# Retention, expert routing and two MLPs on one core: conversion steps, gate halves and weight splits in another order

## The chip, the cores and the metric

One core of a Trainium2 chip runs the whole program. The engines are PE (matrix products; PEld is its loading of weights), DVE (vectors, reads matmul results), ACT (scalar functions and copies), POOL (GpSimd; elementwise work and indirect DMAs) and SP (issues the other DMAs). Each engine runs its own instructions in the order in which the program wrote them, and waits for others through semaphores. The metric is the device time of the program in microseconds (us), the median of several runs; lower is better.

## The reference

```
scores = q @ k^T / 8                      # 8 batches, 8 heads, 576 positions, width 64
x = (scores * D) @ v                      # D[i, j] = gamma_h ** (i - j) for i >= j, else 0; no softmax
logits = x @ w_gate                       # x as 4608 tokens x 512; 8 experts
# greedy: pairs (token, expert) by falling logit; a token is taken once, an expert takes 576 tokens
out[mask_e] = relu(x[mask_e] @ w1[e]) @ w2[e]        # each expert, width 1024
h = relu(out @ w_in); result = (h * h) @ w_out       # one MLP for all tokens, width 2048
```

## The kernel before

All of it is float32; a product of high precision is made of three products of split operands (high part, low part).

**Attention** (`attention`) goes over 36 tiles of 128 tokens, `for t in range(NT)`. A tile's work is cut up by hand and written a tile or two ahead of its use: `turn_k(t + 2)` transposes keys on PE into the bank `pr` and ACT copies them out (line 145, `kT`); `scores(t + 1)` makes the scores of the next tile in two banks `sc` (165), which DVE empties as it multiplies by the decay mask (169, `A`; in each ninth tile a memset behind each, 171); `before(t)` and `values(t)` make the tile's result in `px` (197, 205), which ACT copies to `X` (208, written as `big`); `state(t)` updates the running state (179, and on DVE 183 or 185, `S`). POOL scales queries and keys (152, 155).

The **gate** logits of four tiles at a time come from `gate(t0, t1)`, a generator in two halves. The first multiplies by the gate's weights into `pr` (127) and ACT copies the bank to `gs` (130), which has one buffer; the second transposes `gs` on PE into `pr` again (134) and DVE adds the four parts into `L` (135). `pr` is one bank: each user waits until the one before has been copied out.

**Conversion** (`convert`, the generator `filler`): the weights of the last MLP arrive as float64 and are made into float32 in 32 units. One `next(filler)` is a step, and a unit goes through several: the load in step s, three ACT instructions in step s + 2 (561 to 563), three DVE instructions in step s + 3 (567 to 569), the store to DRAM in step s + 5. Each step so works on several units, with one unit's ACT part and another's DVE part in it. The loop takes one step a tile; what is left is done behind attention.

**The router's first part** (`rt.prep(0, 32)`, two halves) is written at tiles 34 and 35; behind the loop stand the gates of tiles 32 to 34 and of tile 35 (the latter in the bank `sp`), and `rt.prep(32, 36)`. `rt.start()` writes ten DVE instructions once, at tile 3 (358 to 361).

**Then** the threshold search for the first expert runs on DVE and PE (398 to 435), while PE turns `X` back and SP stores it to DRAM (`turn_back`, 658 to 662). `pump()` moves the weight stream: it splits one fetched chunk if it may (`raw` into `w1`, `w2`: ACT 628, POOL 629, DVE 630) and issues the fetch of one more; two chunks may be fetched ahead and three split ahead. `pump(True)` only fetches. When the first expert's token list is ready, POOL gathers its rows by index (`gather`, 708, one instruction a block), PE transposes each block (`turn`, 716), and the expert's products start once three of five blocks are turned (`moe`, 802 then 785). Meanwhile PE is given 36 transposes of nothing (896). In `moe(0)` one `pump()` stands behind each of 16 chunks' use.

Of the kernel before, what the change touches and what calls it, by code (L numbers as in the profile page):

```python
# [6 lines left out]
F32 = mybir.dt.float32  # L7
# [8 lines left out]
NT = 36  # L16
# [53 lines left out]
def attention(tc, a, X, idn, rt, filler):  # L70
# [3 lines left out]
    with ExitStack() as c:  # L74
        cn = c.enter_context(tc.tile_pool(name="acn", bufs=1))
        wk = c.enter_context(tc.tile_pool(name="awk", bufs=2))
# [3 lines left out]
        def load(t, w0=0, w1=3):  # L80

            src = a["att"][t].rearrange("p (w g i) -> p w g i", w=3, g=4)
            if w0 == 0:
                T[t] = wk.tile([128, 2, 4, 128], F32, name="qk", bufs=5)
                nc.sync.dma_start(T[t], src[:, :2])
            if w1 == 3:
                V[t] = wk.tile([128, 4, 128], F32, name="v", bufs=4)
                nc.sync.dma_start(V[t], src[:, 2])
# [33 lines left out]
        def gate(t0, t1, bank="pr"):  # L122

            n, o = t1 - t0, 128 * (t0 % 4)
            p = ps.tile([128, 512], F32, name=bank)
            for g in range(4):
                nc.tensor.matmul(p[32 * g:32 * g + 32, :128 * n], wg[:, g, :], X[t0 // 4][:, g, o:o + 128 * n],
                                 start=True, stop=True)
            gs = wk.tile([128, 512], F32, name="gs", bufs=1)
            nc.scalar.activation(gs[:, :128 * n], p[:, :128 * n], AF.Copy)  # L130
            yield
            p = ps.tile([128, 512], F32, name=bank).rearrange("p (t c e) -> p t c e", t=4, c=4)
            for i in range(n):
                nc.tensor.transpose(p[:, i], gs[:, 128 * i:128 * i + 128], idn)
            nc.vector.tensor_reduce(L[:, t0:t1, :], p[:, :n, :, :NE].rearrange("p t c e -> p t e c"),
                                    axis=AX.X, op=OP.add)
            yield

        def turn_k(t):

            p = ps.tile([128, 512], F32, name="pr").rearrange("p (g i) -> p g i", g=4)
            for g in range(4):
                nc.tensor.transpose(p[:, g], T[t][:, 1, g, :], idn)
            K[t] = wk.tile([128, 4, 128], F32, name="kT")
            nc.scalar.activation(K[t], p, AF.Copy)

        def weigh(t):

            ph, d = t % 9, D[t]
            if ph != 0:  # L150
                d["qh"] = wk.tile([128, 4, 128], F32, name="qh")
                nc.gpsimd.tensor_mul(d["qh"], T[t][:, 0], qc[:, ph])
            if ph != 8:
                kh = wk.tile([128, 8, 64], F32, name="kh")
                nc.gpsimd.tensor_mul(kh, T[t][:, 1].rearrange("p g (h d) -> p (g h) d", h=2),
                                     kc[:, ph, :].unsqueeze(2).to_broadcast([128, 8, 64]))
                d["kh"] = kh.rearrange("p (g h) d -> p g (h d)", h=2)
# [42 lines left out]
        def values(t):  # L200
            ph, px = t % 9, P[t]
            for g in range(4):
                for i in range(2):
                    lo, o = 64 * i, 64 * (i ^ g % 2)
                    nc.tensor.matmul(px[o:o + 64, g, :], V[t][:, g, lo:lo + 64], D[t]["A"][i][:, g, :],  # L205
                                     start=(ph == 0), stop=True)
            o = 128 * (t % 4)
            nc.scalar.activation(X[t // 4][:, :, o:o + 128], px, AF.Copy)
# [4 lines left out]
        def logits():  # L213
            for t in range(0, 32, 4):
                yield from gate(t, t + 4)
# [7 lines left out]
        for t in range(NT):  # L223
            if t + 2 < NT:
                turn_k(t + 2)
            if t + 1 < NT:
                weigh(t + 1)
                scores(t + 1)
            if t + 5 < NT:
                load(t + 5, 0, 2)  # L230
            if t + 3 < NT:
                load(t + 3, 2, 3)
            if t + 2 < 9:
                decay(t + 2)
            before(t)
            if t >= 4 and t % 2 == 0:
                next(todo, None)
            values(t)
            if t % 9 != 8:
                state(t)  # L240
            if t == NT - 2:
                ready = rt.prep(0, 32)
            if t >= NT - 2:
                next(ready)
            if t == 3:
                rt.start()
            next(filler, None)
        last = [gate(32, 35), gate(35, 36, "sp")]
        for g in last:
            next(g)  # L250
        for g in last:
            next(g)
        for _ in rt.prep(32, 36):
            pass

# [329 lines left out]
def body(tc, a, out):  # L585
    nc = tc.nc
    with ExitStack() as ctx:
# [10 lines left out]
        with tc.tile_pool(name="cv", bufs=2) as cv:  # L598
            filler = convert(nc, a, cv, wd)
# [4 lines left out]
        wk = ctx.enter_context(tc.tile_pool(name="wk", bufs=2))  # L604
# [6 lines left out]
        ev, near, listed = {}, set(), set()  # L611
# [8 lines left out]
        def pump(fetch_only=False):  # L620

            i = st["split"]
            if i < st["fetched"] and i < st["used"] + 3 and not fetch_only:
                raw = raws.pop(i)
                w1 = wk.tile([128, 2, 512], R, name="w1", bufs=3)
                w2 = wk.tile([128, 2, 512], R, name="w2", bufs=5)
                for w, c in ((w1, raw[:, :512]), (w2, raw[:, 512:])):
                    nc.scalar.activation(w[:, 0], c, AF.Copy)  # L628
                nc.gpsimd.tensor_sub(w1[:, 1], raw[:, :512], w1[:, 0].bitcast(F32))  # L629
                nc.vector.tensor_sub(w2[:, 1], raw[:, 512:], w2[:, 0].bitcast(F32))  # L630
                chunks[i] = (w1, w2)
                st["split"] += 1
            i = st["fetched"]
            if i < len(stream) and i < st["split"] + 2:
                kind, k, f = stream[i]
                if kind == "e" and k not in ev:
                    return
                raw = raws[i] = wk.tile([128, 1024], F32, name="raw", bufs=2)
                nc.sync.dma_start(raw, wd[f] if kind == "m"
                                  else a["we"][bass.ds(ev[k], 1), f].rearrange("o p c -> (o p) c"))  # L640
                st["fetched"] += 1
# [103 lines left out]
        def route():  # L745
            for k in range(NE):
                yield from rt.phase(k)

        router, loader = route(), load_tokens()
# [138 lines left out]
        while 0 not in listed:  # L888
            long = next(router) == "long"
            for _ in range(1 + long):  # L890
                next(turner, None)
            pump(0 not in near)
        assert next(turner, None) is None
        warm = ps.tile([128, 512], F32, name="mm", bufs=3)
        for _ in range(36):
            nc.tensor.transpose(warm[:, :128], idn, idn)
        while state["turned"] < 3:
            next(loader)
        pump()
# [27 lines left out]
```

## Time and profile before

| | us |
|---|---|
| three runs: lowest, median, highest | 1529.21, 1531.27, 1531.87 |
| the profiled execution's own time | 1525.86 |
| its span | 1524.1 |
| PE busy of the span | 1462.2 (96%) |
| DVE, ACT, POOL busy | 963.5, 675.0, 468.5 |
| attention, up to the last copy to `X` | 0 to 169.5 |
| search for the first expert's list, `X` stored | about 172 to 206 |
| first gather issued; first expert product | 208.19; 218.00 |
| first expert (two parts of 8 chunks) | 218 to 280 |

A row of the timeline is one or some equal instructions: start, duration, engine, line, operation, what it writes and reads, and in brackets how long its engine sat idle before it and what ended that. A row of groups gives the count, the summed busy time and the mean in ns of one. A row of windows gives the busy time of each engine in a stretch, the granted share of TensorE's clock (1.00 is 2.4 GHz, 0.50 is 1.2 GHz) and what the DMA engines moved.

### The profile page before, as it was taken

The page shows a single profiled execution, that of the slowest core. Times are in us where ns is not written, and L with a number is a line of the kernel's source. Part 1 is how long each engine was busy: PE and PEld are TensorE (multiplying, and loading weights), DVE is VectorE, ACT ScalarE, POOL GpSimd, SP SyncE. Part 2 cuts the span into 40 slices and gives each one's busy share as a digit, 9 for nine tenths or more (in the row PEclk, how much of TensorE's full clock was granted, in tenths as well). Part 3 has the DMA queues.
Part 4 walks back from the last instruction along what each step waited for, and adds up shares of the span by engine and source line. Part 5 has one row for each costly group of instructions (what it writes and reads, how often), then busy time and mean ns, then how long its engine had stood idle before and what let it go on. Part 6 is the DMA issues. An engine that isn't in the chain of part 4 may idle for free.

```text
span 1524.1 us, 27399 instructions
## 1 busy us (share of the span) xinstructions
PE 1462.2 (96%) x10599; PEld 1324.4 (87%) x10599; DVE 963.5 (63%) x1965; ACT 675.0 (44%) x1349; POOL 468.5 (31%) x410
## 2 busy tenths in 40 slices
PE   7998879999999999999999999999999999999997
PEld 6777768888988898889988899899888999999896
DVE  5999768766765657557765667567646455454341
ACT  6766644444433434334433344344334344444332
POOL 4454134544312224124213143233122431242110
PEclk9999979999999999999999999999999999999999
DMA  9999567224511224225313143234112351252110
GB/s 337 347 365 352 197 203 257 97 70 133 158 56 72 87 93 154 70 97 157 107 56 96 58 148 127 68 123 161 56 61 89 123 174 64 64 180 95 57 49 21
DMA packets 64210, 201.14 MB, mean 132 GB/s; under 512 B 8400, under 2 KB 8656, under 8 KB 64080
## 3 DMA queue, kind: packets, MB, share of 16 engines
q1 hardware_dynamic: 58128, 179.99, 35.2%
q0 software_dynamic: 5952, 19.40, 3.6%
q8 instruction: 83, 1.36, 0.4%
q14 instruction: 47, 0.39, 0.1%
HBM read 172.10 MB, written 27.26 MB: 131 GB/s over the span
## 4 chain that ended last, share of the span: by engine, by line
PE 73%; DVE 11%; DMA 6%; issue 5%; ACT 4%; POOL 0%; SPq 0%; ACTq 0%; DVEq 0%; POOLq 0%
PE mm L865 24%; PE acc L849 23%; PE acc L785 9%; PE mm L802 8%; DMA raw<-we 4%; DVE w L630 3%; PE px L205 2%; ACT w L628 1%; PE sc L165 1%; PE mm L716 1%; PE rps L508 1%; DVE cb L569 1%; DVE G L398 1%; DVE A L169 1%; DMA raw<-wd 1%
## 5 line engine op out<-in xcount | busy, mean ns | idle before, releaser
L629 POOL TENSOR_TENSOR w<-raw,w 128x512 fp32r<-128x512 f32 x212 | 278.0, 1311 | 825.8 <-ACT w L628 729.0
L630 DVE TENSOR_TENSOR w<-raw,w 128x512 fp32r<-128x512 f32 x212 | 265.4, 1252 | 228.7 <-ACT w L628 224.4
L628 ACT ACTIVATE w<-raw 128x512 fp32r<-128x512 f32 x424 | 243.3, 621 | 205.7 <-DMA raw<-we 163.0
L849 PE MATMUL acc<-big,h 128*128 128x512 f32 x972 | 246.0, 397 | 0.0
L785 PE MATMUL acc<-h,w 128*128 128x288 f32 x1536 | 224.4, 296 | 12.0 <-DVE YL L792 9.7
L785 PEld LDWEIGHTS acc<-h,w 128*128 128x128 f32 x1536 | 208.4, 188 | 14.6 <-DVE YL L792 11.6
L849 PEld LDWEIGHTS acc<-big,h 128*128 128x128 f32 x972 | 180.1, 188 | 35.4 <-DVE h L842 0.3
L871 ACT ACTIVATE r<-mm 128x384 f32<-128x384 f32 x192 | 93.9, 489 | 237.7 <-PE mm L865 217.2
L875 ACT ACTIVATE h<-r 128x384 fp32r<-128x384 f32 x192 | 100.9, 525 | 216.8 <-DVE r L873 216.8
L849 PE MATMUL acc<-w,h 128*128 128x512 f32 x756 | 190.9, 396 | 2.9 <-DVE h L842 2.9
L873 DVE TENSOR_TENSOR r<-mm,r 128x384 f32<-128x384 f32 x192 | 105.9, 551 | 125.5 <-ACT r L871 125.3
L865 PE MATMUL mm<-YH,big 128*128 128x384 f32 x864 | 173.4, 342 | 0.0
L849 PEld LDWEIGHTS acc<-w,h 128*128 128x128 f32 x756 | 139.3, 188 | 29.6 <-DVE h L842 3.7
L802 PE MATMUL mm<-XH,w 128*128 128x288 f32 x1024 | 161.0, 300 | 0.8 <-ACT XH L724 0.7
L865 PEld LDWEIGHTS mm<-YH,big 128*128 128x128 f32 x864 | 152.1, 188 | 7.7 <-ACT YH L791 0.9
L842 DVE TENSOR_TENSOR h<-r,h 128x384 fp32r<-128x384 f32 x192 | 110.9, 577 | 65.7 <-ACT h L875 65.7
L802 PEld LDWEIGHTS mm<-XH,w 128*128 128x128 f32 x1024 | 143.8, 190 | 2.0 <-ACT XH L724 1.1
L865 PE MATMUL mm<-YH,w 128*128 128x384 f32 x672 | 133.3, 339 | 0.0
L865 PEld LDWEIGHTS mm<-YH,w 128*128 128x128 f32 x672 | 117.6, 188 | 4.3
L865 PE MATMUL mm<-YL,big 128*128 128x384 f32 x432 | 93.4, 338 | 0.0
L802 PE MATMUL mm<-XL,w 128*128 128x288 f32 x512 | 89.0, 295 | 0.0
L865 PEld LDWEIGHTS mm<-YL,big 128*128 128x128 f32 x432 | 77.3, 188 | 0.3 <-DVE YL L792 0.2
(171 smaller groups left out, 1713.5 us busy)
## 6 DMA issues: line engine op xcount, KB each, us to landing
raw<-we SPq DMA_DIRECT2D x128, 512.0 KB, 3.6
raw<-wd SPq DMA_DIRECT2D x84, 512.0 KB, 3.2
qk<-att SPq DMA_DIRECT2D x36, 512.0 KB, 7.0
craw<-wm SPq DMA_DIRECT2D x32, 512.0 KB, 6.7
v<-att SPq DMA_DIRECT2D x36, 256.0 KB, 5.4
wd<-cb SPq DMA_DIRECT2D x32, 256.0 KB, 5.4
xd<-YH SPq DMA_DIRECT2D x18, 256.0 KB, 3.5
xd<-YL SPq DMA_DIRECT2D x18, 256.0 KB, 3.6
```

Of the source, the lines that this page charges most:

```text
L205: nc.tensor.matmul(px[o:o + 64, g, :], V[t][:, g, lo:lo + 64], D[t]["A"][i][:, g, :], start=(ph == 0), stop=True)
L628: nc.scalar.activation(w[:, 0], c, AF.Copy)
L629: nc.gpsimd.tensor_sub(w1[:, 1], raw[:, :512], w1[:, 0].bitcast(F32))
L630: nc.vector.tensor_sub(w2[:, 1], raw[:, 512:], w2[:, 0].bitcast(F32))
L785: nc.tensor.matmul(acc[part][d][:, :288], w2[:, wi, d * 128:(d + 1) * 128], h[:, xi, :288], start=(f == 0 and i == 0), stop=(f == 7 and i ...
L802: nc.tensor.matmul(p[:, :288], w1[:, wi, g * 128:(g + 1) * 128], X[xi][:, g, 288 * part:288 * part + 288], start=(g == 0 and i == 0), stop ...
L842: nc.vector.tensor_sub(h[:, 1], s, h[:, 0].bitcast(F32))
L849: nc.tensor.matmul(acc[t], h[:, xi, t * 128:(t + 1) * 128], w2[:, wi], start=(f == 0 and i == 0), stop=(f == 15 and i == 2))
L865: nc.tensor.matmul(p[:, :384], w1[:, wi, g * 128:(g + 1) * 128], Y[xi][:, g, o:o + 384], start=(g == 0 and i == 0), stop=(g == 3 and i == 2))
L871: nc.scalar.activation(r, p[:, :384], AF.Relu)
L873: nc.vector.tensor_mul(s, p[:, :384], r)
L875: nc.scalar.activation(h[:, 0], s, AF.Copy)
```

## The change

```diff
-            gs = wk.tile([128, 512], F32, name="gs", bufs=1)
+            gs = wk.tile([128, 512], F32, name="gs", bufs=2)
...
             before(t)
-            if t >= 4 and t % 2 == 0:
+            if t >= 4 and t % 4 < 2:
                 next(todo, None)
+            if t == NT - 1:
+                last = gate(32, 35)
+                next(last)
             values(t)
             if t % 9 != 8:
                 state(t)
-            if t == NT - 2:
+            if t == NT - 3:
                 ready = rt.prep(0, 32)
-            if t >= NT - 2:
+            if NT - 3 <= t < NT - 1:
                 next(ready)
+            if t == NT - 1:
+                next(last)
             if t == 3:
                 rt.start()
-            next(filler, None)
-        last = [gate(32, 35), gate(35, 36, "sp")]
-        for g in last:
-            next(g)
-        for g in last:
-            next(g)
+            for _ in range(1 + (t in (12, 20, 28))):
+                next(filler, None)
+        for _ in gate(35, 36, "sp"):
+            pass
         for _ in rt.prep(32, 36):
             pass
...
             for _ in range(1 + long):
                 next(turner, None)
-            pump(0 not in near)
+            pump(True)
         assert next(turner, None) is None
         warm = ps.tile([128, 512], F32, name="mm", bufs=3)
         for _ in range(36):
             nc.tensor.transpose(warm[:, :128], idn, idn)
+        for _ in range(4):
+            next(loader)
+        pump()
         while state["turned"] < 3:
             next(loader)
         pump()
```

Tiles 12, 20 and 28 take two conversion steps. With the change the last ACT part of the conversion is written at tile 30 (before: 33), the last DVE part at tile 31 (34), the last store at tile 33 (behind the loop). A gate's second half stands one tile behind its first (before: two), so at tiles 5, 9, ... 33 (6, 10, ... 34). The gate of tiles 32 to 34 has its first half ahead of `values(35)` and its second behind it. The first two chunks of weights are no longer split ahead of the gathers: the first split stands behind four gathers, the second behind three turned blocks, and in `moe(0)` each chunk is then split one chunk later than before.

ACT at tiles 20 and 21, before (208 copies tile 20's result, 561 to 563 are a unit's conversion, 145 copies the keys of tile 23, the next 208 is tile 21):

```order
L130 ACTIVATE gs<-pr 128x512
L208 ACTIVATE big<-px 128x4x128
L561 ACTIVATE cb<-craw 128x512
L562 ACTIVATE cn<-craw 128x512
L563 ACTIVATE cn<-cn 128x512
L145 ACTIVATE kT<-pr 128x512
L208 ACTIVATE big<-px 128x4x128
```

The same place with the change, whose conversion lines are numbered three higher:

```order
L130 ACTIVATE gs<-pr 128x512
L208 ACTIVATE big<-px 128x4x128
L564 ACTIVATE cb<-craw 128x512
L565 ACTIVATE cn<-craw 128x512
L566 ACTIVATE cn<-cn 128x512
L564 ACTIVATE cb<-craw 128x512
L565 ACTIVATE cn<-craw 128x512
L566 ACTIVATE cn<-cn 128x512
L145 ACTIVATE kT<-pr 128x512
L208 ACTIVATE big<-px 128x4x128
```

A second unit stands ahead of the keys' copy out of `pr`, which the gate's second half of tile 21 now follows on PE in the same bank.

DVE from the state of tile 20 to that of tile 21, with the change (570 to 572 are 567 to 569 of before, where one conversion stood and no 135):

```order
L185 TENSOR_TENSOR S_129<-sp,S_128 128x256
L570 TENSOR_SCALAR cs<-cb 128x512
L571 SCALAR_TENSOR_TENSOR cs<-cb,cs 128x512
L572 ISA cb<-cs,cn 128x1024
L570 TENSOR_SCALAR cs<-cb 128x512
L571 SCALAR_TENSOR_TENSOR cs<-cb,cs 128x512
L572 ISA cb<-cs,cn 128x1024
L169 TENSOR_TENSOR A_1710<-sc_1700,mask 128x512
L171 MEMSET A_1710 64x4x64
L169 TENSOR_TENSOR A_1711<-sc_1701,mask 128x512
L171 MEMSET A_1711 64x4x64
L135 TENSOR_REDUCE L<-pr 128x32
```

Two conversions now stand ahead of the masks that empty the score banks, and the gate's addition behind them.

POOL from the last query scaling of attention on, as a difference (629, now 632, is a chunk's subtraction into `w1`; 708, now 711, a gather):

```order
 L152 TENSOR_TENSOR qh<-qk,qc 128x512
-L629 TENSOR_TENSOR w_3213<-raw,w_3213 128x512
-L629 TENSOR_TENSOR w_3243<-raw,w_3243 128x512
-L708 DMA xg<-xd,idx 128x512
-L708 DMA xg<-xd,idx 64x512
-L708 DMA xg<-xd,idx 128x512 x3
```

The same place with the change:

```order
L152 TENSOR_TENSOR qh<-qk,qc 128x512
L711 DMA xg<-xd,idx 128x512
L711 DMA xg<-xd,idx 64x512
L711 DMA xg<-xd,idx 128x512 x2
L632 TENSOR_TENSOR w_3280<-raw,w_3280 128x512
L711 DMA xg<-xd,idx 128x512
L632 TENSOR_TENSOR w_3311<-raw,w_3311 128x512
```

The two subtractions that stood ahead of the gathers have moved behind the fourth and the fifth.

## Rows read from the trace of the kernel before

**Rows 1.** Windows by stage: attention, wait for the gathers, first expert

```profile
25.00:150.00 125.00, 115.58 (x1876) 92.14 (x1868) 114.83 (x188) 88.71 (x164) 65.42 (x51) 1.00 0.98 350
...
198.00:218.00 20.00, 11.43 (x91) 9.70 (x89) 11.54 (x38) 5.03 (x10) 7.89 (x7) 0.69 0.62 204
218.00:276.00 58.00, 53.67 (x401) 51.27 (x402) 51.80 (x114) 28.36 (x57) 26.57 (x19) 0.96 0.59 205
```

**Rows 2.** Timeline of PE, keys' transposes in tiles 20 and 21

```profile
103.97 0.66 PE L143 MATMUL pr<-idn,qk 128*128 128x128 f32 x4
...
107.74 0.66 PE L143 MATMUL pr<-idn,qk 128*128 128x128 f32 x4
```

**Rows 3.** Groups by line on DVE, 20 to 172 us

```profile
L169 DVE TENSOR_TENSOR A<-sc,mask 128x512 f32<-128x512 f32 x66 | 42.3, 677 | 2.7 <-PE sc L165 2.7
...
L569 DVE CUSTOM_DVE_ANT_0 cb<-cs,cn 128x1024 uint16<-128x1024 uint16 x32 | 29.9, 936 | 4.4 <-ACT kT L145 0.5
L567 DVE TENSOR_SCALAR cs<-cb 128x512 int32<-128x512 int32 x32 | 26.0, 811 | 0.0
L568 DVE SCALAR_TENSOR_TENSOR cs<-cb,cs 128x512 int32<-128x512 int32 x32 | 22.1, 692 | 1.1
```

**Rows 4.** Timeline of ACT in tile 20, conversion and keys' copy

```profile
104.12 0.67 ACT L561 ACTIVATE cb<-craw 128x512 f32<-128x512 f32 x1
...
105.97 0.58 ACT L145 ACTIVATE kT<-pr 128x512 f32<-128x512 f32 x1
```

**Rows 5.** Timeline of DVE, first and last instruction of `rt.start()`

```profile
27.40 0.27 DVE L358 MEMSET OH<- 128x256 uint32 x1
...
30.21 0.17 DVE L361 CAST OH<-rt 128x32 f16<-128x32 f32 x1
```

**Rows 6.** Timeline of PE, the scores behind that burst

```profile
33.77 1.75 PE L165 MATMUL sc<-qk,kT 64*128 64x128 f32 x16 [1.00 <-DVE A L169]
```

**Rows 7.** Timeline of PE, behind the gate's second half at tile 30

```profile
149.44 0.66 PE L143 MATMUL pr<-idn,qk 128*128 128x128 f32 x4 [1.70 <-DVE L L135]
```

**Rows 8.** Timeline of PE, gate of tiles 32 to 34, first half

```profile
168.73 0.85 PE L127 MATMUL pr<-big,wg 128*32 128x384 f32 x8
```

**Rows 9.** Timeline of ACT, the copy of tile 35's gate

```profile
170.84 0.28 ACT L130 ACTIVATE gs<-sp 128x128 f32<-128x128 f32 x1 [0.70 <-PE pr L134]
```

**Rows 10.** Timeline of POOL, subtractions, first and third gather

```profile
204.92 2.97 POOL L629 TENSOR_TENSOR w<-raw,w 128x512 fp32r<-128x512 f32 x2 [42.38 <-DVE OH L502]
208.19 1.13 POOL L708 DMA_INDIRECT xg<-xd,idx  x1 [0.30 <-DVE U L523]
...
210.86 0.97 POOL L708 DMA_INDIRECT xg<-xd,idx  x1 [0.30 <-issue]
```

**Rows 11.** Timeline of DVE, index copies and a chunk's subtraction

```profile
206.88 1.03 DVE L514 TENSOR_TENSOR idx<-ids 128x4 int32<-128x4 f32 x1
207.83 0.14 DVE L515 TENSOR_TENSOR idx<-ids 64x1 int32<-64x1 f32 x1
...
209.09 0.69 DVE L630 TENSOR_TENSOR w<-raw,w 128x512 fp32r<-128x512 f32 x1
```

**Rows 12.** Timeline of PE from the idle transposes to the first expert

```profile
205.73 5.79 PE L896 MATMUL mm<-idn 128*128 128x128 f32 x36
211.93 0.66 PE L716 MATMUL mm<-idn,xg 128*128 128x128 f32 x4 [0.40 <-DMA xg<-xd,idx]
...
216.22 1.09 PE L716 MATMUL mm<-idn,xg 128*128 128x128 f32 x4 [0.92 <-DMA xg<-xd,idx]
218.00 2.29 PE L802 MATMUL mm<-XH,w 128*128 128x288 f32 x8 [0.69 <-ACT XH L724]
```

**Rows 13.** Windows: the stretch in which the clock was halved

```profile
216.00:222.80 6.80, 5.89 (x24) 5.51 (x25) 4.00 (x8) 2.71 (x6) 1.28 (x1) 0.50 0.20 57
```

**Rows 14.** Timeline of POOL, subtraction of the sixth chunk's `w1`

```profile
231.39 1.30 POOL L629 TENSOR_TENSOR w<-raw,w 128x512 fp32r<-128x512 f32 x1 [3.98 <-ACT w L628]
```

**Rows 15.** Timeline of PE, the sixth chunk's first products

```profile
236.18 1.30 PE L802 MATMUL mm<-XH,w 128*128 128x288 f32 x8
```

## The prediction, written before the changed kernel had run

> **What bounds the kernel now.** I read the windows by stage first, to see which engines are full where the change lies. In the body of attention PE is busy 115.58 of 125 us and DVE 114.83 [rows 1]: both 92%, so neither has time to give away. PE's own timeline then says what a tile costs it: from one transpose of keys to the next in a tile without gate work are 107.74 - 103.97 = 3.77 us, with its five groups of matmuls back to back [rows 2]. DVE needs as much: a conversion is 0.81 + 0.69 + 0.94 = 2.44 us, two masks are 1.35, together 3.79, and the state's update comes on top [rows 3]. So attention is a loop of PE and DVE in which both are the bound, and only tiles with gate work, where PE takes longer, give DVE a pause. Between 198 and 218 us the picture turns: PE is busy 11.43 of 20 us, part of it with transposes of nothing, and waits for the gathers [rows 1, 12]. From 218 to 276 us the first expert uses its 16 chunks, 58 / 16 = 3.6 us each, PE 93% and DVE 89% busy [rows 1]. Behind that PE is 96% busy over the whole span, and I take every microsecond won or lost ahead of it to be kept to the end.
>
> **Double conversion steps (tiles 12, 20, 28): +7.2.** Nothing is added in all; three conversions move from tiles 32 to 34 forward. In each of the three tiles DVE has one conversion more, 2.44 us [rows 3], ahead of the masks that empty the score banks, and PE's next scores wait for these. ACT has one more too, ahead of the copy of the keys out of `pr`: from the conversion's start to the keys' copy are 105.97 - 104.12 = 1.85 us [rows 4], so the gate's second half, now in the very next tile and in the same bank, finds `pr` taken 1.85 us longer. This wait lies beside DVE's and I don't count it again. A bound from below comes from the one burst of extra DVE work that the trace has: `rt.start()` keeps DVE from 27.40 to 30.38, 3.0 us, and PE's scores behind it waited 1.00 us [rows 5, 6]; a tile with a first gate half stood between. The upper bound is the conversion and the keys' transpose, which now has to wait for the gate's addition behind the masks and comes out in series with the scores: 2.44 + 0.66 = 3.1 us [rows 2, 3]. I take 2.4 for each, nearer to the upper end, since ACT and DVE are late in the same tile: 3 x 2.4 = 7.2, bounds 3.0 and 9.3. What hides a part is DVE's pause in a first-half tile, and all three are such tiles.
>
> **The tiles that lose their conversion (32 to 34): 0.** DVE gets lighter there, but a tile costs PE 3.77 us all the same. Bounds: nothing, and one conversion's 2.44 us gained. The loads and stores of the three units move too; the DMA engines were 98% occupied in the body of attention at 350 GB/s [rows 1], but loads are issued several tiles ahead, so I take nothing for this.
>
> **Second gate halves one tile sooner: -1.7 and +0.6.** At tile 30 DVE's addition stood behind two masks and two memsets, and PE's next transpose waited 1.70 us [rows 7]. The second half moves to tile 29, without memsets: -1.7. Against it, tiles with gate work now stand in pairs, and so do those without. Two plain tiles in a row leave DVE behind PE (3.79 and an update against 3.77): between 0 and some 0.3 us for each of four groups of four tiles that have no double step; half of it, +0.6.
>
> **The end of attention: +0.1.** The gate of tiles 32 to 34 now stands on PE ahead of `values(35)`; its 0.85 us [rows 8] used to lie beside ACT's copy of tile 35 and now delays that copy. In exchange tile 35's gate no longer waits 0.70 us for the one buffer [rows 9]. The router's halves on DVE move to tiles 33 and 34, where there is room, and I count nothing for them. Up to here 7.2 - 1.7 + 0.6 + 0.1 = **+6.2 us**.
>
> **Gathers ahead of the splits: -3.3.** POOL's two subtractions last until 204.92 + 2.97 = 207.89, and the first gather follows at 208.19 [rows 10]. The index copies were done at 207.97, but late: one of them took 1.03 us beside these subtractions, the next, alone, 0.14, and a chunk's subtraction on DVE stood ahead of them [rows 11]. The last matmuls of the list end about when the idle transposes start, 205.73 [rows 12]; with four short copies behind them the first gather can go at about 206.7 (an estimate from the 0.14 and the 0.30 that POOL takes from one gather to the next), 1.5 us sooner. What counts is the third gather, since the expert starts with three blocks. It came 2.67 us behind the first, so now at 209.4, and leaves POOL at 210.3. PE turned the first block 2.6 us behind POOL's end (211.93 - 209.32) and the third 4.4 us (216.22 - 211.83) [rows 10, 12]; the fetches of two more chunks, issued as the splits freed their buffers, ran beside it, and these now come later. With 2.6 the third block turns at 212.9, by when the idle transposes (to 211.52) and two turns are over: 3.3 us sooner, and the expert's first product with it, at 214.7 for 218.00. With 4.4 it is 1.5. If the turn also runs as fast as the first one (0.66 for 1.09 us) it is 3.7. I take 3.3.
>
> One rule speaks against this part. The split's subtraction on DVE now runs while POOL issues gathers; in the trace before it did so too, at 209.09 for 0.69 us, and the first gather took 1.13 us where the third took 0.97 [rows 10, 11], so 0.16 is the price seen. The Trainium skill, "SBUF — State Buffer", section "Who interferes with whom", says that an instruction of DVE with two SBUF inputs and one of GpSimd that reads SBUF exclude each other for their whole length; by that the index copy's 1.03 us is explained, and a gather could be held for the whole 0.69 us, the gain would be 2.6 and the sum +3.9.
>
> **Weights one chunk later in the first expert: +0.3.** The sixth chunk's `w1` was ready at 231.39 + 1.30 = 232.69 and used at 236.18, 3.5 us ahead [rows 14, 15]; one chunk takes 3.6. So the weights arrive about when PE wants them. The whole chain of splits starts as much sooner as the expert does. I take 0.3; bounds 0, and 3 if PE waits for weights in most chunks.
>
> **Sum.** +6.2 - 3.3 + 0.3 = **+3.2 us**. The profiled execution took 1525.86, 5.4 below the median of the runs shown; on that median it is 1531.27 + 3.2 = **1534.5 us**.
>
> **Rivals.** *The double steps are absorbed* (the other side). If DVE's pause in the first-half tile takes up most of the second conversion, as the burst suggests, a double step costs 1.0: 3.0 - 1.7 + 0.1 = 1.4, and with -3.3 - 1.6 for the expert's start the result is -3.5, 1527.8. The 1.6 is the clock: it fell to 0.50 from 216 to 222.8 us [rows 13], after PE had mostly waited for gathers, and the turn of the third block took 1.09 for 0.66 us [rows 12]. With less waiting it may not fall; the first expert's products from 218.00 on stood in that stretch, and half of its 6.8 us is 3.4, of which DVE's own work leaves perhaps half. For it: that burst. Against it: the burst cost 1.00 with a pause on both sides, and ACT is late as well. The point that decides is whether a double step costs PE under 1.5 us. The Trainium skill, "TensorE: Matmul & The Clock Gate", section "Why this matters for your kernels", asks for no long idle gaps between matmuls to keep the high clock; the fall at 216 agrees with it, and by it this rival's 1.6 us would come. Chance 0.17.
>
> *The weights are late* in the first expert: the start of the expert moves, its end doesn't, since each chunk now has one use less of lead. Then the 3.3 us are lost and the result is +6.2, 1537.5. For it: 3.5 us of lead against 3.6 for a chunk. Against it: the fetches are issued by the splits and start sooner too. Chance 0.13.
>
> *Nothing changes*: double steps at about 1.5 and a gain of 1.5 to 3.3 at the gathers cancel, 1531 to 1532. Chance 0.12.
>
> **Chances and range.** The forecast, between 0 and +6.5, holds 0.58; its own range is 1531.5 to 1537.5. What a measurement can tell from no change is about 0.2%, 3.1 us, and the forecast lies on that bound: of its 0.58 I give 0.33 to slower and 0.25 to the same. With the late weights slower has 0.46, with the third rival and a little of the first the same has 0.39, faster has 0.15. The range reaches to the first and second rival: 1527.5 to 1539.
>
> **What would show it.** PE idle of some 2 us in tiles 13, 21 and 29, ended by DVE's masks or the gate's addition or ACT's keys; the 1.70 us of tile 30 gone; the last copy to `X` some 6 us later than before; the first gather about 1.5 us closer to the end of the list's matmuls and the expert's product 9 us behind them for 12.3; no wait of PE for `w1`. It would be wrong if DVE's pauses hide the second conversions, or if the weights set the pace of the first expert.

## The result, and the profile after

The changed kernel takes 1537.89 us (median of 9 runs, 1534.44 to 1540.77), the kernel before 1529.54 beside it (9 runs, 1522.35 to 1533.53): ratio 1.0057, 95% interval 1.0038 to 1.0076, so **slower by 8.4 us** (5.8 to 11.6). The forecast was 3.2 us slower, with a range to 1539.0: right in sign and inside the range, short by 5 us.

The profiled execution of the changed kernel took 1540.16 us, with a span of 1538.4. That is 14.3 above the span of before, far more than the medians differ: the first profile of before lies near the low end of its kernel's times. A second profile of the same kernel, taken later (it is the last experiment below), has a span of 1532.6. Both stand in the tables from here on, and what differs between these two is no work of the change.

The windows by stage of the changed kernel answer to [rows 1]. Columns after the stretch: its length, the busy time of PE, PEld, DVE, ACT and POOL, the granted clock, the DMA share, GB/s.

```profile
25.00:150.00 125.00, 111.85 (x1770) 89.19 (x1768) 113.56 (x182) 88.21 (x162) 62.72 (x48) 0.97 0.95 341
208.00:226.00 18.00, 10.83 (x93) 9.60 (x92) 10.38 (x38) 3.94 (x8) 6.32 (x6) 0.81 0.56 184
226.00:286.00 60.00, 54.22 (x401) 51.91 (x402) 52.21 (x113) 27.01 (x57) 25.68 (x19) 0.94 0.63 210
```

In the same 125 us of attention PE's instructions are 1770 for 1876, and the clock is 0.97 for 1.00: attention lost time, and part of that by the clock. The first expert behind it runs at 0.94 for 0.96. What each stage took, in us, from the start of the row that ends it to that of the next (last copy of the normalised tokens to `X`; end of the list's last matmul; first product of the first expert; end of its last L802, L805 after; first product of the second expert, which ends the first shared MLP; end of the span):

| Stage ends with | before | before, second profile | after |
| --- | --- | --- | --- |
| last copy to `X` | 168.9 | 170.4 | 178.6 |
| list's last matmul | 37.0 | 36.9 | 38.4 |
| first product, expert 1 | 12.1 | 11.8 | 8.9 |
| last first-layer product, expert 1 | 57.7 | 62.3 | 59.8 |
| first product, expert 2 | 83.0 | 83.4 | 86.9 |
| end | 1165.4 | 1167.8 | 1165.7 |

Attention is 8.2 to 9.7 longer, the way from the list to the expert 2.9 to 3.2 shorter, the stage that holds the first shared MLP 3.5 to 3.9 longer. The 1.4 us more up to the list's last matmul are not charged to the change: this profile has 0.50 from 182.26 to 189.09 us there, and all other profiles take 36.1 to 37.6. Four groups of rows carry the rest of the text.

**A double step.** ACT and PE behind tile 20, timelines of the changed kernel. ACT copies the second conversion's words, waits for DVE (0.52), and comes to the copy of the keys at 112.77:

```profile
110.36 0.65 ACT L564 ACTIVATE cb<-craw 128x512 f32<-128x512 f32 x1
111.53 0.67 ACT L565 ACTIVATE cn<-craw 128x512 f32<-128x512 uint16 x1 [0.52 <-DVE cb L572]
112.24 0.63 ACT L566 ACTIVATE cn<-cn 128x512 int32<-128x512 f32 x1
112.77 0.58 ACT L145 ACTIVATE kT<-pr 128x512 f32<-128x512 f32 x1
```

```profile
110.08 0.67 PE L197 MATMUL px<-qh,S 64*64 64x128 f32 x16
113.41 0.66 PE L134 MATMUL pr<-idn,gs 128*128 128x128 f32 x4 [2.66 <-ACT kT L145]
113.99 1.98 PE L205 MATMUL px<-A,v 128*64 128x128 f32 x16
115.75 1.07 PE L179 MATMUL sp<-v,kh 128*64 128x64 f32 x16
```

PE, which in [rows 2] goes from one tile to the next without a pause, waits 2.66 us for those keys, since the gate's second half wants their bank. And behind the wait the same 16 matmuls of L205 take 1.98 us, where they take 1.09 elsewhere in attention. Windows of the granted clock behind the three double steps of this kernel (columns as above):

```profile
76.45:79.86 3.41, 3.41 (x38) 2.96 (x34) 2.60 (x6) 1.79 (x4) 0.87 (x1) 0.50 0.78 284
114.00:117.41 3.41, 3.41 (x36) 3.29 (x36) 2.83 (x8) 1.39 (x3) 0.43 (x1) 0.50 0.94 366
151.54:154.96 3.42, 3.42 (x36) 3.00 (x34) 2.12 (x5) 0.70 (x2) 0.00 (x0) 0.50 0.78 308
```

At 0.50 of 2.4 GHz, 3.4 us do the work of 1.7.

**The gathers.** POOL and PE of the changed kernel, timelines, for [rows 10, 12]:

```profile
218.33 1.26 POOL L711 DMA_INDIRECT xg<-xd,idx  x1 [46.71 <-DVE nn L530]
219.89 0.91 POOL L711 DMA_INDIRECT xg<-xd,idx  x1 [0.30 <-issue]
221.10 0.97 POOL L711 DMA_INDIRECT xg<-xd,idx  x1 [0.30 <-issue]
```

```profile
216.85 5.56 PE L899 MATMUL mm<-idn 128*128 128x128 f32 x36
222.25 1.17 PE L719 MATMUL mm<-idn,xg 128*128 128x128 f32 x8
224.60 0.63 PE L719 MATMUL mm<-idn,xg 128*128 128x128 f32 x4 [1.18 <-DMA xg<-xd,idx]
225.91 1.71 PE L805 MATMUL mm<-XH,w 128*128 128x288 f32 x8 [0.69 <-ACT XH L727]
```

From the start of the idle transposes to the third block's turn are 7.75 us for 10.49 (10.58 in the second profile of before). That turn takes 0.63 for 1.09, but 0.63 in the second profile of before too, so this part is no effect of the change. The first gather, with the split's subtraction on DVE beside it (218.60, 0.69 us), takes 1.26 where the next two take 0.91 and 0.97: some 0.3 us, and not the 0.69 that the prediction drew from the Trainium skill, "SBUF — State Buffer", "Who interferes with whom". The same section also says that a `tensor_tensor`, which this subtraction is, was not seen to stall DMAs; the 0.3 us lie between the two.

**The first shared MLP.** DVE and PE of the changed kernel, timelines:

```profile
296.86 1.38 DVE L633 TENSOR_TENSOR w<-raw,w 128x512 fp32r<-128x512 f32 x1 [1.63 <-ACT w L631]
298.16 1.64 DVE L845 TENSOR_TENSOR h<-r,h 128x384 fp32r<-128x384 f32 x1
...
302.68 1.36 DVE L633 TENSOR_TENSOR w<-raw,w 128x512 fp32r<-128x512 f32 x1 [1.64 <-ACT w L631]
303.97 1.62 DVE L845 TENSOR_TENSOR h<-r,h 128x384 fp32r<-128x384 f32 x1
```

```profile
299.86 1.90 PE L852 MATMUL acc<-big,h 128*128 128x512 f32 x7 [0.82 <-DVE h L845]
...
305.64 1.89 PE L852 MATMUL acc<-w,h 128*128 128x512 f32 x7 [1.21 <-DVE h L845]
```

A chunk's subtraction (L633) stands ahead of the low half of the activations (L845), and PE's second layer waits for that, twice. Both are long here: POOL's subtractions of the same split and of a kept chunk of the last MLP's weights lie beside them (296.39 to 299.38), and where POOL subtracts nothing L633 takes 0.69 (218.60) and L845 0.56 (306.65). In the kernel before, PE's timeline shows no wait in the same steps (276 to 300 us). Splits are made while they lead by less than three chunks; the changed kernel enters this stage with a lead of two, so its first step, which takes a chunk that was kept in SBUF and so uses up none of the stream, makes one split more.

### The profile page after: what moved, and what is told of

It is laid out like the page before. It is cut to its first block, busy times and chain, and to the rows that moved or that the text cites. A ratio compares the mean times of both kernels' runs of the same rounds, so it can differ in the third digit from the quotient of the medians.

```text
span 1538.4 us, 27395 instructions
## 1 busy us (share of the span) xinstructions
PE 1468.5 (95%) x10599; PEld 1330.9 (87%) x10599; DVE 966.9 (63%) x1965; ACT 674.6 (44%) x1349; POOL 468.4 (30%) x410
## 4 chain that ended last, share of the span: by engine, by line
PE 69%; DVE 13%; DMA 7%; issue 5%; ACT 4%; POOL 0%; SPq 0%; ACTq 0%; DVEq 0%; POOLq 0%
PE mm L868 24%; PE acc L852 23%; PE acc L788 6%; PE mm L805 6%; DMA raw<-we 6%; DVE w L633 4%; PE px L205 2%; ACT w L631 2%; PE sc L165 1%; DVE G L401 1%; PE rps L511 1%; PE mm L719 1%; DVE cb L572 1%; PE mm L661 1%; PE pr L143 1%
## 5 line engine op out<-in xcount | busy, mean ns | idle before, releaser
L633 DVE TENSOR_TENSOR w<-raw,w 128x512 fp32r<-128x512 f32 x212 | 267.6, 1262 | 232.1 <-ACT w L631 226.8
L788 PE MATMUL acc<-h,w 128*128 128x288 f32 x1536 | 225.0, 297 | 15.8 <-DVE YL L795 12.1
L805 PE MATMUL mm<-XH,w 128*128 128x288 f32 x1024 | 161.3, 300 | 0.9 <-ACT XH L727 0.7
L845 DVE TENSOR_TENSOR h<-r,h 128x384 fp32r<-128x384 f32 x192 | 112.0, 583 | 65.0 <-ACT h L878 65.0
L805 PEld LDWEIGHTS mm<-XH,w 128*128 128x128 f32 x1024 | 144.0, 190 | 1.9 <-ACT XH L727 0.9
L805 PE MATMUL mm<-XL,w 128*128 128x288 f32 x512 | 89.1, 296 | 0.0
```

Source lines behind the costliest of these rows:

```text
L788: nc.tensor.matmul(acc[part][d][:, :288], w2[:, wi, d * 128:(d + 1) * 128], h[:, xi, :288], start=(f == 0 and i == 0), stop=(f == 7 and i ...
L805: nc.tensor.matmul(p[:, :288], w1[:, wi, g * 128:(g + 1) * 128], X[xi][:, g, 288 * part:288 * part + 288], start=(g == 0 and i == 0), stop ...
L845: nc.vector.tensor_sub(h[:, 1], s, h[:, 0].bitcast(F32))
```

## The experiments

Each was timed in five rounds against the kernel before on the same chip; the ratios are to that, and microseconds are the ratio times 1531. L numbers shift with the lines of each kernel.

**Single steps, all else as changed.**

```
-            for _ in range(1 + (t in (12, 20, 28))):
+            for _ in range(1):
```

> The change with one conversion step in every tile, all else as in the change. Theory: the double steps are the whole loss; each costs some 3.7 us, 2.7 of them PE's wait for the keys' copy and the rest the halved clock behind that wait. Without them attention's last copy to X comes at about 169, as before, PE's clock stays at 1.00 in attention, and the kernel is 3 to 4 us faster than before, some 11 us faster than the change. Rival: the doubles cost the 2.4 us each that was forecast and the rest comes from the search and the first expert; then this kernel stays 2 to 3 us slower than before.

Ratio 1.0011 [0.9995, 1.0027]. Against the changed kernel's 1.0057 the double steps are worth 7.0 us, with some 4 us to either side. No stretch at half clock stands in attention before 168 us. Stages: 171.1, 37.6, 8.8, 58.8, 86.5, 1166.3. The expected gain of 3 to 4 us over the kernel before didn't come, though the way from the list to the expert took 8.8 us.

**Gathers ahead of the splits alone** (the second part of the diff on the kernel before).

> The kernel before with the gathers ahead of the weight splits alone. Theory: the first expert's product comes 3 us sooner after the list's last matmuls (9.0 for 12.1 us), and the gain is kept: 3 us faster than before, 1527 for 1530. Rival, late weights: the first expert's end does not move or comes later, since each chunk is split one chunk later; then within 1 us of before, or up to 4 us slower, as the second half of the first expert in the profile after (4 us longer than before) would have it.

Ratio 1.0012 [0.9995, 1.0029]: no gain, so the time is the rival's, but not for its reason, since the first expert is not longer. Stages: 170.5, 36.9, 8.9, 55.6, 86.1, 1167.0. Its first product comes 3.2 us closer to the list, and the first expert keeps that; the clock is 1.00 from the expert's first product on, and the first eight matmuls take 1.32 us for the 2.29 of [rows 12]. But the MLP's stage is 3 us longer, by the same two waits. PE's timeline of this kernel at both places:

```profile
216.35 1.32 PE L802 MATMUL mm<-XH,w 128*128 128x288 f32 x8 [0.69 <-DVE XL L725]
...
285.17 1.90 PE L849 MATMUL acc<-big,h 128*128 128x512 f32 x7 [0.82 <-DVE h L842]
290.96 1.90 PE L849 MATMUL acc<-w,h 128*128 128x512 f32 x7 [1.22 <-DVE h L842]
```

**The attention part alone** (the changed kernel with splits and gathers as before).

> The change with the weight splits ahead of the gathers as before, so the attention part alone. Theory: all of the loss is here, 9 to 11 us slower than before, more than the whole change (8 us). Rival: about 6 us slower, with the rest of the loss in the first expert, and so no slower than the change.

Ratio 1.0048 [1.0032, 1.0065], 7.4 us. Stages: 176.3, 37.2, 11.7, 61.7, 83.5, 1165.6. That lies between the two expectations. So the loss is attention's. Its code there is the changed kernel's, and PE waits as long behind tile 12; but L205 behind the wait takes 1.09 us, and the clock holds (timeline of PE, then windows of 72 to 80 us):

```profile
76.41 0.66 PE L134 MATMUL pr<-idn,gs 128*128 128x128 f32 x4 [2.69 <-ACT kT L145]
77.00 1.09 PE L205 MATMUL px<-A,v 128*64 128x128 f32 x16
```

```profile
72.00:76.00 4.00, 1.73 (x33) 1.36 (x32) 3.70 (x5) 3.39 (x7) 2.91 (x2) 1.00 1.02 381
76.00:80.00 4.00, 3.22 (x48) 2.75 (x50) 3.88 (x7) 2.18 (x5) 1.04 (x1) 1.00 0.97 312
```

That gives a double step's price without the clock: up to tile 31 this kernel stands 8.2 us behind the next one, which has the same gate and single steps, and 0.7 of that is there before the first double; so 2.5 us for each.

**The gate's part alone** (the changed attention with single steps; splits and gathers as before).

> The kernel before with the regrouped gate alone: second halves in the tile behind the first half, tiles 32 to 34 prepared one tile sooner, gs in two buffers; no double steps, gathers and weight splits as before. By the prediction's terms this is -1.7 (second halves), +0.6 (keys copied later) and +0.1 (end), together -1.0: ratio 0.9993, last copy of the normalised tokens about 168 us against 168.9 of before. Rival: the end of attention is worth more than the 0.1 taken for it, since single steps with these gates ended attention 2.2 us later than before: last copy at about 171, ratio 1.001 to 1.002. If this ratio and that of single steps with the gathers ahead (1.0011) are alike, then the gathers gain nothing whatever stands ahead of them.

Ratio 1.0005 [0.9988, 1.0022]. Stages: 171.1, 37.2, 10.7, 60.5, 83.1, 1167.8. The regrouping gains only at tile 30: its copy of tile 27 to `X` comes 0.7 us later than in the first profile of before, that of tile 31 comes 0.8 us sooner. But the last four tiles take 19.1 us for 16.0, so the last copy comes at 171, where the rival had it. DVE and PE, timelines:

```profile
163.52 0.42 DVE L377 TENSOR_TENSOR V<-V,rt 128x256 f32<-128x256 f32 x1
163.86 0.42 DVE L570 TENSOR_SCALAR cs<-cb 128x512 int32<-128x512 int32 x1
...
166.94 0.41 DVE L185 TENSOR_TENSOR S<-sp,S 128x256 f32<-128x256 f32 x1
```

```profile
167.50 0.67 PE L197 MATMUL px<-qh,S 64*64 64x128 f32 x16 [2.09 <-DVE S L185]
168.09 1.07 PE L127 MATMUL pr<-big,wg 128*32 128x384 f32 x8
169.09 1.97 PE L205 MATMUL px<-A,v 128*64 128x128 f32 x16
```

The router's half, one tile sooner, and a conversion stand ahead of the state's update, PE waits 2.09 us, and behind the wait, at 0.50 (168.60 to 172.01), L205 takes 1.97 for 1.09: of the 3 us some 1.5 are the longer wait and 0.9 the clock in this row. With double steps that conversion is gone: the changed kernel waits 0.62 there, as before, and its last four tiles take 16.1.

**Double steps alone** (`for _ in range(1 + (t in (12, 20, 28)))` on the kernel before).

> The kernel before with the double conversion steps at tiles 12, 20, 28 and nothing else; its gate halves stand two tiles apart, so no gate half lies in the tile behind a double step. If a double costs what it adds on DVE ahead of the next scores (2.44 us): last copy of the normalised tokens 7 us later than before, ratio 1.0045. If what it collides with decides (in the changed kernel the gate's second half lies behind it and PE waits 2.7 us for the copy of the keys, and the granted clock halves): PE's waits stay below 2 us, attention at full clock, last copy 3 to 5 us later, ratio 1.002 to 1.003.

Ratio 1.0065 [1.0045, 1.0086], 10.0 us: dearer without a gate half behind them, not cheaper. Attention takes 185.4 in its profile (then 37.0, 11.0, 59.9, 83.5, 1165.7). PE's timeline behind tile 12:

```profile
75.58 0.66 PE L143 MATMUL pr<-idn,qk 128*128 128x128 f32 x4 [2.39 <-ACT kT L145]
77.06 2.67 PE L165 MATMUL sc<-qk,kT 64*128 64x128 f32 x16 [0.82 <-DVE A L169]
79.67 1.13 PE L197 MATMUL px<-qh,S 64*64 64x128 f32 x16
80.73 1.11 PE L134 MATMUL pr<-idn,gs 128*128 128x128 f32 x4
81.77 1.98 PE L205 MATMUL px<-A,v 128*64 128x128 f32 x16
```

PE waits for ACT's keys and again for DVE's masks, and then the clock is at 0.50 from before 78 to past 84 us. Behind the other two doubles it waits 1.20 and 1.75 us, again with 6.8 us at 0.50. The changed kernel waits once, for 2.65 to 2.69 us, and has 3.4 us at 0.50. The theory that the gate's second half makes the price falls.

**Double steps at tiles 14, 22, 30**, all else as changed.

> The changed kernel with its double conversion steps at tiles 14, 22, 30 instead of 12, 20, 28, so that no second half of the gate follows in the next tile. If a double step costs what it adds on DVE ahead of the next scores (the prediction's 2.4 us each), it costs the same here: ratio to before 1.005 to 1.006, last copy 7 to 8 us later than before. Rival: the cost lies in PE's wait of 2.7 us for the copy of the keys out of the bank that the gate shares with them, and in the halved clock behind that wait: then the wait shrinks to about 1 us or is gone, no stretch at 0.50 stands in attention, last copy 3 to 5 us later, ratio about 1.002.

Ratio 1.0105 [1.0092, 1.0119], 16.1 us: both expectations missed. PE waits 2.40 and 0.82 behind the first double, as in the experiment before, 1.2 and 1.8 behind the others, and at the first the half clock (87.26 to 94.08 us) falls on the gate's first half too. Stages: 185.5, 37.1, 8.9, 59.6, 87.8, 1168.6.

**Double steps at tiles 13, 21, 29**, all else as changed.

> The changed kernel with the double steps one tile later, at 13, 21, 29, so that their additional work falls into tiles 14, 22, 30, behind both halves of the gate and ahead of none for one more tile. With doubles two tiles later attention grew by 16 us, since the additional work came just ahead of the gate's first half, and PE waited, and ran at half clock behind the wait. If the price is what a double meets: last copy 3 to 6 us later than with single steps, ratio to before 1.002 to 1.004, no stretch at 0.50 in the body of attention. If each double costs its own work wherever it stands: 7 us, ratio 1.0045 to 1.006 as in the changed kernel.

Ratio 1.0073 [1.0047, 1.0098], runs from 1535.73 to 1550.85, the profile being the slowest: 185.4, 36.2, 8.8, 61.1, 87.1, 1170.3. PE waits twice behind each double here too, 2.6 to 3.0 us in all, and half clock follows all three; the first expectation missed, and the 7 us of the second lie at the lower edge of the interval. No place tried is shown to be cheaper than the change's own.

**A third split behind the gathers** (one more `pump()` ahead of the expert, in the changed kernel).

> The change with one more pump before the first expert, so that three chunks are split when it starts, as before. If the weights' smaller lead costs the 4 us of the first expert's second half, this is 3 to 4 us faster than the change. If that stretch is long for another reason (the clock, DVE's order), it is the same as the change within 1 us, or slower by 1 us as the first product waits for ACT's third split.

Ratio 1.0052 [1.0031, 1.0072], the same as the change, as the second expectation had it. Stages: 179.7, 37.2, 8.9, 61.4, 83.6, 1165.0. The MLP's stage is back at 83.6, so the third chunk of lead is what it wants; but the first expert pays for it: counted from the list, its first product comes when it does in the change, 8.9 us, but the first chunk's second layer at some 20 us, for 15 to 16 in the other kernels with gathers ahead, and half clock lies there (231.6 to 238.4 us).

**A lead of two, filled late** (gathers ahead, on the kernel before).

```
-            if i < st["fetched"] and i < st["used"] + 3 and not fetch_only:
+            if i < st["fetched"] and i < st["used"] + (3 if st["used"] > 22 else 2) and not fetch_only:
```

> The kernel before with gathers ahead of the splits, and the splits held to a lead of two chunks (instead of three) until the first 23 chunks are used, so that no additional split falls into the first steps of the first shared MLP stage. Theory from the traces: the first product is 3.2 us sooner, and what took it back is one more split in that stage's second step, whose subtraction on VectorE (1.37 us) stands ahead of the low half of h, so that PE waits 0.8, 1.2 and 0.2 us more. Held back, the give-back is gone: first product of the second expert stage 3.0 to 3.4 us sooner than before, ratio 0.9978 to 0.9985. Rival: the lead itself was what is needed, and with one chunk less the stage waits for its weights elsewhere: ratio 1.000 or above, with waits of PE for w on the split.

Ratio 0.9996 [0.9982, 1.0009]; stages 170.3, 36.9, 8.9, 56.8, 85.3, 1167.6. The two waits at the start of the MLP are gone, as expected: its last step still starts 2.7 us sooner than before. But where the lead is then filled, PE waits twice, for 1.39 and 2.15 us (timeline):

```profile
351.97 1.89 PE L849 MATMUL acc<-w,h 128*128 128x512 f32 x7 [1.39 <-DVE h L842]
356.47 1.89 PE L849 MATMUL acc<-big,h 128*128 128x512 f32 x7 [2.15 <-DVE h L842]
```

Before has one of 1.45 there, and the second is new. The split costs nearly the same where it now falls, 2.3 us, and the ratio lies between the two expectations.

**The same lead with the changed gate and single steps.**

> The changed kernel without its double steps and with the splits held to a lead of two in the same way: regrouped gate, gathers ahead of splits, no additional split in the first shared MLP stage. By the theory from the traces: single steps with the gathers ahead (ratio 1.0011) less the give-back of 2.6 to 3.5 us: ratio 0.9985 to 0.999. If the regrouped gate gains its 1.0 us as well, this is the fastest of all: ratio 0.997 to 0.998. Rival as for the lead held without the gate's part: 1.000 or above.

Ratio 1.0007 [0.9998, 1.0016]: no gain, as the rival had it; here too 2.3 us are lost where the lead is filled. Stages: 171.1, 36.1, 8.8, 62.2, 86.5, 1168.8.

**A lead of two to the end** (`i < st["used"] + 2`, gathers ahead, on the kernel before).

> The kernel before with gathers ahead of the splits, and a lead of two split chunks to the end (it is never filled to three). With the lead held until the end of the first shared MLP stage its give-back was gone there (2.75 us sooner than before up to its last step), but the additional split came at the end of that stage, and PE waited 2.3 us more there. Theory: a split costs 2.3 to 2.6 us of PE's time wherever it falls inside a stage, and one that never comes keeps the gain: first product of the second expert stage 2.5 to 3.4 us sooner than before, ratio 0.998 to 0.9985. Rival: the third chunk of lead covers something in the later stages, and the time comes back there: ratio 0.9995 to 1.001.

Ratio 0.9990 [0.9974, 1.0007]. Stages: 169.4, 37.0, 8.9, 57.1, 84.0, 1170.9. The second expert starts 2.4 us sooner than before, as the theory had it; then later experts give it back, the second 1.7 us and the fifth 4.1 within their first eight chunks (3.4 us at 0.50 lie in the fifth). The ratio lies between the theory's and the rival's and doesn't decide. In the second, PE waits for the split itself (timeline):

```profile
368.83 0.80 PE L802 MATMUL mm<-XH,w 128*128 128x288 f32 x4 [0.57 <-POOL w L629]
```

**The kernel before, against itself.**

> The kernel before, unchanged: a second profile of it, and what a comparison of a kernel with itself gives. Ratio 1.000 with an interval of about 0.0015 to each side. Its profile shows which differences between stages belong to the run: if the stretches at half clock stand elsewhere, its milestones differ from those of the first profile by 1 to 4 us without any change.

Ratio 0.9989 [0.9974, 1.0003], as far from 1 as the best experiment. Its span is 8.5 us above that of the first profile; the largest piece, 4.6 us, is the first expert's stage. DVE there, with POOL's subtractions at 257.73 and 258.96 beside it, then PE and the windows of 256 to 270 us of the first and of this profile:

```profile
257.72 1.33 DVE L437 TENSOR_SCALAR k<-kf,B 128x36 f32<-128x36 f32 x1
259.08 1.20 DVE L438 SCALAR_TENSOR_TENSOR k<-k,kf 128x36 f32<-128x36 f32 x1
```

```profile
257.73 1.28 POOL L629 TENSOR_TENSOR w<-raw,w 128x512 fp32r<-128x512 f32 x1 [1.39 <-ACT w L628]
258.96 1.26 POOL L688 TENSOR_TENSOR big<-big 128x512 fp32r<-128x512 f32 x1
```

```profile
262.06 3.25 PE L785 MATMUL acc<-h,w 128*128 128x288 f32 x12 [3.77 <-DVE YL L792]
```

```profile
256.00:270.00 14.00, 11.92 (x96) 11.23 (x95) 12.69 (x28) 6.72 (x14) 7.86 (x6) 1.00 0.39 137
```

```profile
256.00:270.00 14.00, 10.22 (x64) 9.77 (x63) 11.07 (x26) 5.45 (x13) 5.07 (x5) 0.76 0.42 135
```

Two small instructions of DVE that took 0.24 and 0.20 us in the first profile take 1.33 and 1.20, until POOL's subtractions end; PE then waits 3.77 us for 1.72, and within that wait, at 260.23, the clock falls. The changed kernel has the same picture at 261.95 (1.32 and 1.20, PE waiting 3.91): since an unchanged kernel can have it, that part of its first expert can't be charged to the change.

## Why the prediction was right or wrong

The forecast holds in sign and inside its range, and is short by 5 us. It is partly luck that the measured time lies inside: it is near the upper end, which a rival had set whose reason did not come. With +7.4 for attention and about -0.5 for the gathers, as found below, the sum would have been about 6.9, inside the measured 5.8 to 11.6.

**Where it failed: the step "gathers ahead of the splits: -3.3", with the rule that every microsecond won ahead of the first expert is kept to the end.** Its mechanism and its size at the place were right. In all nine kernels with gathers ahead the first product stands 8.8 to 8.9 us behind the list, in the others 10.7 to 12.1; the first gather follows the list's last matmul by 1.3 us for 2.3 (1.0 us sooner, where 1.5 was expected), and PE turns the third block 2.5 us behind POOL's end for 4.4. But moved alone it gained nothing that can be measured (+1.8 us, -0.8 to +4.4). What the splits had cost ahead of the gathers is work that has to be done somewhere: with two splits made ahead of the expert instead of three, one more falls into the first shared MLP, and PE waits some 2.7 us more (by the shift of the steps 1.1, 1.5 and 0.2, in the kernel with this part alone). These three shifts stand at the same steps, to within 0.1 us, in all five kernels that enter this stage with a lead of two and fill it there, and in none of the five profiles that, like the first of before, enter it with three, the second of before among them; so they are not the difference between executions. That this split is the cause is shown by holding it back: the waits go, and come where it is made next (2.3 us). With a lead of two to the end the later experts give the gain back. The term should have been about -0.5, about 3.2 gained and 2.7 given back, which the medians can't tell from 0. What a split costs inside a later stage was never bounded, since I took all behind the first expert for PE's alone.

**The double steps, +7.2:** right in size. The changed kernel against the one with single steps gives 7.0 us, with some 4 us to either side. What ends PE's wait is other than I put first: the keys' copy on ACT, behind a second conversion that itself waits for DVE, rather than DVE's masks. At full clock a double costs 2.5 us, as the 2.4 had it. Where the clock falls behind the wait it is 3.5 in the changed kernel (10.4 us up to tile 31, against single steps) and 5 to 5.5 in the profile of doubles alone (against the two profiles of before); that price I had only on the gathers' side.

**The tiles that lose their conversion, 0, and the end of attention, +0.1.** The changed kernel's last four tiles take 16.1 us for 16.0, as said. But the two terms belong together: with the new places of gate and router and with the conversions still there they take 19.1. So the doubles buy 3 us at the end and pay 10 in front; at full clock it is some 7.5 in front, and less than 3 at the end, since part of the 19.1 is half clock.

**Second gate halves, -1.7 and +0.6:** the 1.70 us of tile 30 are gone in the changed kernel, and the gate's part alone stands 0.8 us sooner at tile 31, for -1.1 expected; of the whole part 0.8 us (-1.8 to +3.4) is all that the medians tell. The term for attention, +6.2, is +7.4 measured.

**Weights later, +0.3.** No wait of PE for `w1` shows in the first expert of the changed kernel. The rival "weights late" named the right loss, the lead, and the wrong place: not in the first expert, and not by late weights, but by the split's work one stage on. Its 1537.5 came closest for a reason that isn't its own.

**The doubles absorbed, and nothing changes:** neither came. A double cost PE more than the 1.5 us that decided. (The first rival's sum also left out the +0.6 and the +0.3 of the forecast, without a reason.) Its bonus, that the clock would hold behind quicker gathers, didn't come in the profile of the changed kernel: the granted clock is 0.50 at 212.99 to 219.81 and 226.64 to 230.05. But it came in most others. In seven of the nine profiles with gathers ahead the clock is 1.00 over the first 10 us of the expert, in four of the five without it is 0.76 to 0.85; the forecast's own sum had left this gain out, and no experiment prices it alone. The Trainium skill, "TensorE: Matmul & The Clock Gate", "Why this matters for your kernels", asks for no long gaps between matmuls. Here half clock stands behind waits of 2.65 to 2.69 us in the changed kernel, and behind 1.69 and 2.09 in single profiles of others, all shorter than the gap named there, while in the changed attention alone a wait of 2.69 has 1.00 behind it: a shorter wait was enough in some executions and not in others.

Still open: what of the gathers' gain remains under the noise of the medians; and why one wait is followed by a half clock and the same wait in another execution is not.

## What to carry to other kernels

Work taken off the way of one wait is not gone: before a gain is counted to the end, find the place where that work is done instead, and price it there by what then waits for it. A wait that a moved step adds costs more than its length where the clock falls behind it, so a step that costs 2.4 us by its busy time can cost 3.5 or 5. And take two profiles of the kernel before: here they lay 8.5 us apart, as much as the whole effect, and part of one stage's loss in the changed kernel stands in an execution of the kernel before too.

## What the runs showed that I had not expected

The same program falls to half clock in one execution and not in another. In the first profile of before, PE waits 1.70 us at tile 30 [rows 7], and the clock stays at 1.00; in the second it waits 1.69, and L205, three groups on, takes 1.97 us (timeline of the second profile):

```profile
149.55 0.66 PE L143 MATMUL pr<-idn,qk 128*128 128x128 f32 x4 [1.69 <-DVE L L135]
...
152.44 1.97 PE L205 MATMUL px<-A,v 128*64 128x128 f32 x16
```

A fall costs half its length where PE is the bound. The second profile of before has 33.4 us at 0.50 in its span, the first 24.7, so falls can account for up to 4.3 of the 8.5 us between them; the rest is not traced.

A small instruction of DVE can be held for a whole subtraction of POOL's, 1.33 and 1.20 for 0.24 and 0.20 us, which agrees with the Trainium skill, "SBUF — State Buffer", "Who interferes with whom", by which the shared pair of ports is an exclusive lock. Which instruction is hit changes from one execution to the next: in the first profile of before it is one of the pair of L398 behind them (the pair takes 1.96 us for 0.95). With it changes PE's wait, 1.72 or 3.77 us.
